# A fused attention and mixture-of-experts kernel: running sums of one-hot vectors moved to TensorE, a cast to GpSimd, an exponential to an earlier step

## The chip, the cores and the metric

The kernel runs on one core of one Trainium2 chip. The metric is the device time of one execution in microseconds (us). A core has five engines with instruction queues of their own: TensorE (PE; its weight loads are listed as PEld), VectorE (DVE), ScalarE (ACT), GpSimd (POOL) and SyncE (SP, which issues most DMAs here). Instructions of one engine start in program order, and engines wait for each other through semaphores.

## The reference

Attention with a bias learned from relative positions, for 8 batches of 8 heads with 576 tokens of 64 channels, then a mixture of 8 experts in which every one of the 4608 tokens goes to the expert with the highest logit.

```python
def _attn_ref(q, k, v, w1, b1, w2):                 # q, k, v: 8 x 8 x 576 x 64
    scores = scale * np.matmul(q, k.transpose(0, 1, 3, 2))
    ...
    bias = np.maximum(x @ w1 + b1, 0.0) @ w2        # x: log distance over log position
    scores = scores + bias.transpose(2, 0, 1)[None, :, :, :]
    attn = np.exp(scores - np.max(scores, axis=-1, keepdims=True))
    attn = attn / (np.sum(attn, axis=-1, keepdims=True) + 1e-09)
    return np.matmul(attn, v)

def _moe_ref(x, modality_id, w_gate, modality_bias, w1, w2):   # x: 4608 x 512
    logits = x @ w_gate + modality_bias[modality_id]
    e_idx = np.argmax(logits, axis=1)
    probs = np.exp(logits - logits.max(-1, keepdims=True))
    probs /= probs.sum(-1, keepdims=True) + 1e-09
    gate_w = probs[np.arange(N), e_idx]
    for e in range(E):                              # 8 experts, 512 -> 1024 -> 512
        mask = e_idx == e
        h = np.maximum(x[mask] @ w1[e], 0.0)
        out[mask] = gate_w[mask, None] * (h @ w2[e])
```

## The kernel before

The program has three phases: a bias table, the attention, and the expert tiles. The attention goes through 32 pairs of heads, four pairs to a batch. One iteration of `attention` over a pair `n` is called a step below; it has five units (`u` = 0 to 4), one per block of 128 query rows (the last block holds the remaining 64 rows of both heads). A unit begins with its score matmuls (`S`: L402 on TensorE); VectorE then adds the bias and takes the row minimum (L416, once per head, into `Eb`), ScalarE does the softmax exponentials (L431), TensorE transposes them (L446), VectorE or ScalarE copies the transposes out (L333, L331, into `eT`), and TensorE multiplies by the values (L500, L491). The next pair's queries and keys are prepared on the way: VectorE transposes them (L378), ScalarE rounds them (L385), and GpSimd subtracts to get the remainder (L386, into `QK`), which the next step's score matmuls read.

The order of everything is written by hand, as the strings of `ORDER`, one letter for an operation, one string for a unit. The letters `X` and `B` stand for the next operation of a queue of background work. After the four pairs of a batch are done, this background work is the batch's routing (`route_steps`), 576 tokens at a time: five groups of up to 128 tokens, 8 experts. Its list `px` (letter `X`) has logits, their transposes, the rank and five times a row scatter; its list `ot` (letter `B`) has reciprocals, the maximum (`s_top`), the one-hot vectors (`s_onehot`), the gate (`s_gate`) and the positions (`s_pos`). A routing so takes about one batch's four steps. Seven of the eight routings run in the attention; the eighth runs beside the first expert tiles (`moe_first`).

Three of these functions, in the order in which they are issued, are touched by the change, and a fourth:

- `s_onehot`, issued at the end of a step's second unit. VectorE makes `oh`, the one-hot vector of each token's expert (L793 to L798, 128 x 5 x 8). GpSimd casts it to bf16 (L801), and VectorE adds up the groups before each group in bf16, five additions of 128 x 8 (L803). Both results stand in `ohb`.
- `s_rank`, in the third unit. TensorE multiplies the cast vectors by a triangular matrix (L816, within a group) and the running sums by ones (L817, groups before). VectorE adds the base of each expert (L820), raises the base (L821) and keeps the entry of the token's own expert (L822).
- `s_gate`, in the third unit. ScalarE exponentiates the logits in place (L807); VectorE adds them up and inverts (L809 to L811) and copies the token numbers (L812).
- `s_pos`, at the start of the fourth unit. VectorE adds over the experts (`pf`, L828) and casts to int32 (`pos`, L830). `s_rows` then transposes 128 rows (L838), copies, scales (L845) and scatters them by `pos` with an indirect DMA (L849), from the fourth unit on.

Of the kernel before, what the change touches and what calls it, by code (L numbers as in the profile page):

```python
# [11 lines left out]
F32 = mybir.dt.float32  # L12
BF16 = mybir.dt.bfloat16
F32R = mybir.dt.float32r
I32 = mybir.dt.int32
AF = mybir.ActivationFunctionType
ALU = mybir.AluOpType
# [4 lines left out]
P = 128  # L22
# [7 lines left out]
E = 8  # L30
# [78 lines left out]
class Attn:  # L109
# [506 lines left out]
    def route_setup(self, cp):  # L616

        tc, nc, io = self.tc, self.nc, self.io
# [13 lines left out]
        nc.gpsimd.memset(self.rec, 1.0)  # L632
        self.oh = cp.tile([P, 6, E], F32, name="oh")
        nc.gpsimd.memset(self.oh, 0.0)
        self.ohb = cp.tile([P, 2, 6, E], BF16, name="ohb")
        nc.gpsimd.memset(self.ohb, 0.0)
        yield
        self.base = cp.tile([P, E], F32, name="base")
# [59 lines left out]
        for a, (dst, mk) in enumerate(((t0, m1), (self.mbias, mf))):  # L698
# [4 lines left out]
                op=ALU.mult,  # L703
# [4 lines left out]
    def route_steps(self, b):  # L708
        nc, rt = self.nc, self.rt
        xT = [self.xT.pop(NP * b + p) for p in range(NP)]  # L710
        sums = [self.sums.pop(NP * b + p) for p in range(NP)]
        rec, oh = self.rec, self.oh
        C5 = [P, 5, E]
        st = {}

        def bc(t):
            return t.rearrange("p (c o) -> p c o", o=1).to_broadcast(C5)
# [71 lines left out]

        def s_onehot():  # L790
            lg, mx = st["lg"], st["mx"]

            nc.vector.scalar_tensor_tensor(  # L793
                oh[:, 0:5, :], lg, 0.0, self.rev.rearrange("p (o e) -> p o e", o=1).to_broadcast(C5), op0=ALU.is_ge, op1=ALU.mult
            )
            nc.vector.tensor_reduce(mx, oh[:, 0:5, :], axis=AX.X, op=ALU.max)
            nc.vector.tensor_tensor(oh[:, 0:5, :], oh[:, 0:5, :], bc(mx), op=ALU.is_equal)
            nc.vector.tensor_tensor(oh[:, 0:5, :], oh[:, 0:5, :], bc(self.valid), op=ALU.mult)  # L798

            ohb = self.ohb  # L800
            nc.gpsimd.tensor_copy(ohb[:, 0, 0:5, :], oh[:, 0:5, :])  # L801
            for k in range(1, 6):
                nc.vector.tensor_tensor(ohb[:, 1, k, :], ohb[:, 1, k - 1, :], oh[:, k - 1, :], op=ALU.add)  # L803

        def s_gate():
            lg = st["lg"]
            nc.scalar.activation(lg, lg, AF.Exp)  # L807
            gt = rt.tile([P, 5], F32, tag="gt", name=f"gt{b}")
            nc.vector.tensor_reduce(gt, lg, axis=AX.X, op=ALU.add)  # L809
            nc.vector.tensor_scalar(gt, gt, 1e-9, None, op0=ALU.add)  # L810
            nc.vector.reciprocal(self.gi[:, :, 0], gt)  # L811
            nc.vector.tensor_copy(self.gi[:, :, 1], self.ids[:, 5 * b : 5 * b + 5])  # L812

        def s_rank():
            ps = self.xbank()[:, 0 : 6 * E].rearrange("p (c e) -> p c e", e=E)
            nc.tensor.matmul(ps, self.tri, self.ohb[:, 0], start=True, stop=False)  # L816
            nc.tensor.matmul(ps, self.ones, self.ohb[:, 1], start=False, stop=True)  # L817
            rk = rt.tile(C5, F32, tag="rk", name=f"rks{b}")
            bb = self.base.rearrange("p (o e) -> p o e", o=1)
            nc.vector.tensor_tensor(rk, ps[:, 0:5, :], bb.to_broadcast(C5), op=ALU.add)  # L820
            nc.vector.tensor_tensor(self.base, self.base, ps[:, 5, :], op=ALU.add)  # L821
            nc.vector.tensor_tensor(rk, rk, oh[:, 0:5, :], op=ALU.mult)  # L822
            st["rk"] = rk

        def s_pos():
            rk = st["rk"]
            pf = rt.tile([P, 5], F32, tag="pf", name=f"pf{b}")
            nc.vector.tensor_reduce(pf, rk, axis=AX.X, op=ALU.add)  # L828
            pos = rt.tile([P, 5], I32, tag="pos", name=f"pos{b}", bufs=2)
            nc.vector.tensor_copy(pos, pf)  # L830
            st["pos"] = pos

        def s_rows(c):
# [22 lines left out]
            return f  # L856

        px = [(1, s_logits(0)), (1, s_logits(1)), (1, s_logits_t(0)), (1, s_logits_t(1)), (3, s_rank)] + [(5, s_rows(c)) for c in range(5)]
        ot = [(0, s_recip), (4, s_top), (4, s_onehot), (4, s_gate), (5, s_pos)]
        if b == self.B - 1:  # L860
            ot += [(5, f) for f in self.last_tables()]
# [595 lines left out]
```

## Time and profile before

| quantity | value |
|---|---|
| device time, median of 3 runs | 1053.26 us (1050.47 to 1053.33) |
| profiled execution, device time | 1052.45 us |
| its span, first to last instruction | 1050.7 us |
| TensorE busy | 997.9 us, 95% |
| VectorE busy | 764.5 us, 73% |
| ScalarE busy | 666.8 us, 63% |
| GpSimd busy | 304.7 us, 29% |
| mean granted TensorE clock | 0.995 |

The profile is that of one execution. Durations of instructions, waits and the order of events come from it; the other runs give the median. An engine's busy share is a mean over stages that differ, so the stage in question has to be looked at by itself. A matmul's record covers its whole way through the array, so that records of successive matmuls overlap; the distance between two starts tells what one costs.

### The profile page before, as it was taken

The numbers are of one execution on the slowest core, as the hardware profiler recorded it, in microseconds if no ns is written. First come the engines' busy times: TensorE is split into PE (matmuls) and PEld (weight loads), VectorE is DVE, ScalarE is ACT, GpSimd is POOL, SyncE is SP. The second block draws the span as 40 slices with busy tenths as digits, with TensorE's granted clock in tenths as the row PEclk, the third lists the DMA queues.
The fourth block names the chain that finished last, engine by engine and source line by source line (L and its number), as shares of the span: only waits on it lengthen the run. The fifth ranks groups of instructions, "written<-read, shape, count | busy, mean of one in ns | idle before, by whom it ended". The sixth has DMA issues, their size and how long they took to land. (4 is left out here: it accounts for less than half of the span.)

```text
span 1050.7 us, 22872 instructions
## 1 busy us (share of the span) xinstructions
PE 997.9 (95%) x8236; PEld 786.4 (75%) x8236; DVE 764.5 (73%) x1566; ACT 666.8 (63%) x1265; POOL 304.7 (29%) x489
## 2 busy tenths in 40 slices
PE   6789999998999999999999899999999999999997
PEld 2347766776767767676677678988999999898886
DVE  8886678778787786877879767797566676565555
ACT  6777776776767767677677655555455555554544
POOL 1512333525335244253352411441110111111111
PEclk9999999999999999999999999999999999999999
DMA  6977723233334323352325511122215641170610
GB/s 150 191 154 146 189 54 73 68 69 78 72 56 93 66 59 74 55 110 50 79 60 103 166 36 41 61 67 71 61 51 120 220 133 51 41 224 26 226 40 26
DMA packets 247325, 97.50 MB, mean 93 GB/s; under 512 B 207759, under 2 KB 228623, under 8 KB 247203
## 3 DMA queue, kind: packets, MB, share of 16 engines
q1 hardware_dynamic: 241186, 76.92, 32.9%
q0 software_dynamic: 5920, 19.03, 5.0%
q8 instruction: 67, 1.10, 0.4%
q14 instruction: 56, 0.45, 0.1%
q10 hardware_dynamic: 96, 0.00, 0.0%
HBM read 134.90 MB, written 23.90 MB: 151 GB/s over the span
## 5 line engine op out<-in xcount | busy, mean ns | idle before, releaser
L431 ACT ACTIVATE Eb<-Eb,mn 128x576 f32<-128x576 f32 x288 | 221.2, 769 | 66.1 <-DVE mn L416 63.3
L416 DVE CUSTOM_DVE_ANT_0 Eb<-sps,NBm 128x576 f32<-128x576 f32 x256 | 183.6, 754 | 62.2 <-PE sps L402 56.2
L402 PE MATMUL sps<-QK 64*128 64x288 f32 (+1 forms) x1728 | 171.1, 309 | 2.0 <-DVE mn L416 1.7
L402 PEld LDWEIGHTS sps<-QK 64*128 64x128 f32 (+1 forms) x1728 | 133.8, 185 | 45.8 <-DVE mn L416 15.5
L1181 PE MATMUL p<-QK,w1hi 128*128 128x256 f32 x1136 | 161.5, 285 | 1.7 <-DVE QK L1165 0.9
L446 PE MATMUL eps<-idf,Eb 128*128 128x128 f32 x1024 | 147.8, 279 | 10.6 <-DVE eT L333 8.3
L1181 PEld LDWEIGHTS p<-QK,w1hi 128*128 128x128 f32 x1136 | 147.0, 191 | 5.4 <-issue 1.8
L500 PE MATMUL xps<-eT,vraw 128*64 128x288 f32 x1024 | 148.7, 416 | 0.0
L446 PEld LDWEIGHTS eps<-idf,Eb 128*128 128x128 f32 x1024 | 111.2, 141 | 41.8 <-issue 17.8
L1207 POOL DMA_INDIRECT out<-mo,idt x36 | 41.4, 1151 | 301.4 <-ACT mo L1206 228.2
L1184 DVE SCALAR_TENSOR_TENSOR hl<-p,hh 128x512 fp32r<-128x512 f32 x72 | 49.7, 690 | 101.4 <-ACT hh L1183 97.8
L1183 ACT ACTIVATE hh<-p 128x512 fp32r<-128x512 f32 x72 | 43.0, 597 | 122.1 <-PE p L1181 106.7
L331 ACT ACTIVATE eT<-eps 128x512 f32<-128x512 f32 x160 | 94.7, 592 | 34.7 <-PE eps L446 26.3
L1198 PE MATMUL p<-w2hi,hl 128*128 128x512 f32 x288 | 112.4, 390 | 0.3 <-DVE hl L1184 0.3
L1198 PE MATMUL p<-w2hi,hh 128*128 128x512 f32 x288 | 112.4, 390 | 0.0
L436 POOL COPY rem<-Eb 128x128 f32<-128x128 f32 x128 | 37.5, 293 | 249.6 <-ACT Eb L431 246.6
L500 PEld LDWEIGHTS xps<-eT,vraw 128*64 128x64 f32 x1024 | 65.9, 138 | 54.1 <-issue 20.5
L1143 DVE TENSOR_TENSOR w2lo<-NBm,w2hi 128x1024 fp32r<-128x1024 f32 x72 | 88.1, 1224 | 15.9 <-ACT w2hi L1142 15.9
L333 DVE COPY eT<-eps 128x512 f32<-128x512 f32 x128 | 87.1, 681 | 12.0 <-PE eps L446 11.5
L1181 PE MATMUL p<-QK,w1lo 128*128 128x256 f32 x568 | 91.3, 283 | 0.0
L1143 DVE TENSOR_TENSOR w1lo<-NBm,w1hi 128x1024 fp32r<-128x1024 f32 x72 | 83.3, 1220 | 0.0
L1181 PEld LDWEIGHTS p<-QK,w1lo 128*128 128x128 f32 x568 | 78.3, 192 | 0.0
(213 smaller groups left out, 1574.8 us busy)
## 6 DMA issues: line engine op xcount, KB each, us to landing
NBm<-moe_w SPq DMA_DIRECT2D x44, 1024.0 KB
NBm<-moe_w SPq DMA_DIRECT2D x80, 512.0 KB
NBr<-xg SPq DMA_DIRECT2D x80, 128.0 KB
kraw<-k SPq DMA_DIRECT2D x128, 72.0 KB
NBm<-xTb SPq DMA_DIRECT2D x32, 288.0 KB
vraw<-v SPq DMA_DIRECT2D x64, 128.0 KB
NBm<-moe_w SPq DMA_DIRECT2D x3, 2048.0 KB
xg<-blank SPq DMA_DIRECT2D x9, 516.0 KB
```

The source lines that it names most:

```text
L331: self.nc.scalar.activation(out, ps, AF.Copy, scale=scale)
L333: self.nc.vector.tensor_copy(out, ps)
L402: nc.tensor.matmul(self.sps[h][:, half, 0:HS], QK[o, q, qs], QK[o, k, HS * half : HS * half + HS], start=i == 0, stop=i == 2, skip_group_c ...
L416: nc.vector.tensor_tensor_reduce(out=e.rearrange("p (t w) -> p t w", t=2), in0=self.sps[h][:, :, 0:HS], in1=nb.rearrange("p (t w) -> p t w ...
L431: self.nc.scalar.activation(e, e, AF.Exp, bias=mn, scale=-1.0, accum_out=sm)
L446: nc.tensor.transpose(ps[:, k, :], e[:, part, P * k : P * k + P], self.idf)
L500: nc.tensor.matmul(ps[o, :], v[:, h, k, :], self.eT[:, h, k, sl], start=half == 1 and k == 0, stop=half == 0 and k == 3, tile_position=(0, ...
L1143: self.nc.vector.tensor_tensor(l, w, h.bitcast(F32), op=ALU.subtract)
L1181: nc.tensor.matmul(ps[:, a, :], w[:, c, fs], x[:, c, :], start=i == 0, stop=i == len(ops) - 1)
L1183: nc.scalar.activation(hh[:, sl, :], ps, AF.Relu)
L1184: nc.vector.scalar_tensor_tensor(hl[:, sl, :], ps, 0.0, hh[:, sl, :].bitcast(F32), op0=ALU.max, op1=ALU.subtract)
L1198: nc.tensor.matmul(ps, h[:, f, sl], m[:, f, :], start=i == 0, stop=i == len(ops) - 1)
```

## The change

- `ohb` holds the bf16 one-hot vectors alone. VectorE's product with the mask of valid tokens writes them directly; GpSimd's cast and the five additions on VectorE are gone.
- The rank is one product with the triangular matrix and five products with ones: group `k` of the one-hot vectors, repeated by a stride of zero, is added into the results of all later groups, so that the accumulation in PSUM makes the running sums.
- The exponentials of the gate are written to a tile of their own (`eg`), and are issued in `s_onehot`.
- The position cast is GpSimd's instead of VectorE's.

```diff
-        self.ohb = cp.tile([P, 2, 6, E], BF16, name="ohb")
+        self.ohb = cp.tile([P, 6, E], BF16, name="ohb")
...
         def s_onehot():
             lg, mx = st["lg"], st["mx"]
-
+            st["eg"] = eg = rt.tile(C5, F32, tag="eg", name=f"eg{b}")
+            nc.scalar.activation(eg, lg, AF.Exp)
...
-            nc.vector.tensor_tensor(oh[:, 0:5, :], oh[:, 0:5, :], bc(self.valid), op=ALU.mult)
-
-            ohb = self.ohb
-            nc.gpsimd.tensor_copy(ohb[:, 0, 0:5, :], oh[:, 0:5, :])
-            for k in range(1, 6):
-                nc.vector.tensor_tensor(ohb[:, 1, k, :], ohb[:, 1, k - 1, :], oh[:, k - 1, :], op=ALU.add)
+            nc.vector.tensor_tensor(self.ohb[:, 0:5, :], oh[:, 0:5, :], bc(self.valid), op=ALU.mult)
 
         def s_gate():
-            lg = st["lg"]
-            nc.scalar.activation(lg, lg, AF.Exp)
+            lg = st["eg"]
...
         def s_rank():
             ps = self.xbank()[:, 0 : 6 * E].rearrange("p (c e) -> p c e", e=E)
-            nc.tensor.matmul(ps, self.tri, self.ohb[:, 0], start=True, stop=False)
-            nc.tensor.matmul(ps, self.ones, self.ohb[:, 1], start=False, stop=True)
+            ohb = self.ohb
+            nc.tensor.matmul(ps, self.tri, ohb, start=True, stop=False, skip_group_check=True)
+            for k in range(5):
+                nc.tensor.matmul(
+                    ps[:, k + 1 : 6, :],
+                    self.ones,
+                    ohb[:, k : k + 1, :].to_broadcast([P, 5 - k, E]),
+                    start=False,
+                    stop=k == 4,
+                    skip_group_check=True,
+                )
...
-            nc.vector.tensor_tensor(rk, rk, oh[:, 0:5, :], op=ALU.mult)
+            nc.vector.tensor_tensor(rk, rk, self.ohb[:, 0:5, :], op=ALU.mult)
...
-            nc.vector.tensor_copy(pos, pf)
+            nc.gpsimd.tensor_copy(pos, pf)
```

VectorE's queue around the one-hot vectors, before: the end of the second unit, then L416, with which the third unit begins (`mn` and `Eb` are its results).

```order
L333 COPY rT<-eps_717 128x64
L793 SCALAR_TENSOR_TENSOR oh<-lgs_1917,rev 128x40
L796 TENSOR_REDUCE mx_1939<-oh 128x5
L797 TENSOR_TENSOR oh<-oh,mx_1939 128x40
L798 TENSOR_TENSOR oh<-oh,valid 128x40
L803 TENSOR_TENSOR ohb<-ohb,oh 128x8 x5
L416 ISA Eb,mn_2_0_2033<-sps_714,NBm 128x576
```

The same place after the change.

```order
L333 COPY rT<-eps_717 128x64
L794 SCALAR_TENSOR_TENSOR oh<-lgs_1917,rev 128x40
L797 TENSOR_REDUCE mx_1939<-oh 128x5
L798 TENSOR_TENSOR oh<-oh,mx_1939 128x40
L799 TENSOR_TENSOR ohb<-oh,valid 128x40
L416 ISA Eb,mn_2_0_2029<-sps_714,NBm 128x576
```

Five additions have left the queue ahead of L416; nothing else moved there. On the same queue the cast L830, between `pf` (L828) and the fourth unit's L416, is gone too.

GpSimd's queue from the second to the fourth unit, before (`rem` is a copy of the last 64 columns of `Eb`, `QK` the remainders that the next step reads).

```order
L801 CAST ohb<-oh 128x40
L436 COPY rem_1_2015<-Eb 128x128
L386 TENSOR_TENSOR QK_73<-qT,QK_73 128x640
L436 COPY rem_2_2065<-Eb 128x128
L386 TENSOR_TENSOR QK_73<-kT,QK_73 128x576
L845 TENSOR_TENSOR xrb_90<-xrb_90,rec 128x512
```

The same place after the change.

```order
L436 COPY rem_1_2011<-Eb 128x128
L386 TENSOR_TENSOR QK_73<-qT,QK_73 128x640
L436 COPY rem_2_2064<-Eb 128x128
L834 CAST pos_2072<-pf_2070 128x5
L386 TENSOR_TENSOR QK_73<-kT,QK_73 128x576
L849 TENSOR_TENSOR xrb_90<-xrb_90,rec 128x512
```

The cast of the one-hot vectors has left the queue ahead of the query remainder, and the position cast stands now ahead of the key remainder.

## Rows read from the trace of the kernel before

**Rows 1.** The page's first part: busy time, share of the span, instructions.
```profile
PE 997.9 (95%) x8236; PEld 786.4 (75%) x8236; DVE 764.5 (73%) x1566; ACT 666.8 (63%) x1265; POOL 304.7 (29%) x489
```

**Rows 2.** Who waited for whom: total us, times, longest.
```profile
PE xps L817 <- DVE ohb L803: 11.4, 7, 1.6
```

**Rows 3.** Stretches: us, busy of PE, PEld, DVE, ACT, POOL, clock, DMA, GB/s.
```profile
178.33:195.13 16.80, 16.50 (x151) 12.36 (x150) 12.52 (x28) 12.05 (x29) 10.55 (x16) 1.00 0.41 97
...
227.53:246.57 19.04, 16.49 (x149) 12.34 (x148) 17.07 (x49) 12.73 (x31) 5.80 (x9) 1.00 0.33 57
```

**Rows 4.** TensorE's timeline, step with the rank: start, us, then [idle before <-releaser].
```profile
234.13 1.05 PE L402 MATMUL sps<-QK 64*128 64x288 f32 x12
...
236.05 0.19 PE L816 MATMUL xps<-ohb,tri 128*128 128x48 bf16 x1
237.86 0.18 PE L817 MATMUL xps<-ohb,ones 128*128 128x48 bf16 x1 [1.63 <-DVE ohb L803]
...
239.10 1.25 PE L402 MATMUL sps<-QK 64*128 64x288 f32 x12
...
243.17 1.05 PE L402 MATMUL sps<-QK 128*128 128x288 f32 x6
245.14 1.06 PE L446 MATMUL eps<-idf,Eb 128*128 128x128 f32 x8 [0.92 <-DVE eT L333]
```

**Rows 5.** TensorE's timeline in the step from 178.33: fourth and fifth unit.
```profile
188.49 1.05 PE L402 MATMUL sps<-QK 64*128 64x288 f32 x12
...
192.37 1.03 PE L402 MATMUL sps<-QK 128*128 128x288 f32 x6
193.70 1.06 PE L446 MATMUL eps<-idf,Eb 128*128 128x128 f32 x8 [0.30 <-ACT Eb L431]
```

**Rows 6.** Stretch of a third unit with no routing matmul, columns as above.
```profile
201.74:204.88 3.14, 3.14 (x30) 2.17 (x28) 2.31 (x7) 3.02 (x8) 1.78 (x2) 1.00 0.00 0
```

**Rows 7.** VectorE's timeline in the step with the rank.
```profile
235.17 0.20 DVE L798 TENSOR_TENSOR oh<-oh,valid 128x40 f32<-128x40 f32 x1
235.40 2.41 DVE L803 TENSOR_TENSOR ohb<-ohb,oh 128x8 bf16<-128x8 bf16 x5
237.79 0.76 DVE L416 CUSTOM_DVE_ANT_0 Eb<-sps,NBm 128x576 f32<-128x576 f32 x1
...
239.85 0.16 DVE L820 TENSOR_TENSOR rks<-xps,base 128x40 f32<-128x40 f32 x1
...
241.63 0.82 DVE L830 CAST pos<-pf 128x5 int32<-128x5 f32 x1
242.36 0.74 DVE L416 CUSTOM_DVE_ANT_0 Eb<-sps,NBm 128x576 f32<-128x576 f32 x1
```

**Rows 8.** GpSimd's timeline there: both remainders.
```profile
235.85 1.53 POOL L386 TENSOR_TENSOR QK<-qT,QK 128x640 fp32r<-128x640 f32 x1
...
240.99 1.44 POOL L386 TENSOR_TENSOR QK<-kT,QK 128x576 fp32r<-128x576 f32 x1 [0.21 <-ACT QK L385]
```

**Rows 9.** One line's instructions: shortest/median/longest ns, first and last start.
```profile
L803 DVE TENSOR_TENSOR ohb<-ohb,oh x5: 167/168/1468, 235.4 to 237.6; 128x8 bf16<-128x8 bf16 x5
...
L817 PEld LDWEIGHTS <-ones x8: 97/98/100, 167.8 to 650.6; 128*128 128x128 bf16 x8
```

**Rows 10.** Timelines of VectorE and TensorE at the eighth routing.
```profile
649.35 0.98 DVE L803 TENSOR_TENSOR ohb<-ohb,oh 128x8 bf16<-128x8 bf16 x5
...
665.41 0.17 DVE L830 CAST pos<-pf 128x5 int32<-128x5 f32 x1
...
650.58 0.20 PE L816 MATMUL xps<-ohb,tri 128*128 128x48 bf16 x1
650.62 0.18 PE L817 MATMUL xps<-ohb,ones 128*128 128x48 bf16 x1
```

**Rows 11.** ScalarE's timeline in the step with the rank.
```profile
238.59 0.78 ACT L431 ACTIVATE Eb<-Eb,mn 128x576 f32<-128x576 f32 x1 [2.19 <-DVE mn L416]
...
239.37 0.22 ACT L807 ACTIVATE lgs<-lgs 128x40 f32<-128x40 f32 x1
```

## The prediction

> **What bounds the kernel now.** I read the busy shares first. TensorE is busy for 95% of the span [rows 1] and its granted clock in the steps below is 1.00, the 2.4 GHz level [rows 3], so time is to be won only where TensorE stands still. The list of waits names such a place on the lines of this change: the second rank product (L817) waits 11.4 us in 7 waits for VectorE's running sums (L803) [rows 2]. The eighth routing, in the expert phase, has no such wait.
>
> Next I compared the steps of the attention loop. The step from 178.33 and the step from 227.53, which carry different parts of a routing, have the same TensorE time, 16.50 and 16.49 us. They last 16.80 and 19.04 us [rows 3]. The second is the one with the one-hot, rank and position code, and it leaves TensorE idle for 2.55 us. There are seven such steps, one in every four from the seventh step on. A step has five units, each opened by its score matmuls (L402). In this step the third unit lasts 239.10 - 234.13 = 4.97 us, the fourth 243.17 - 239.10 = 4.07, and the fifth, up to the step's end at 246.57, 3.40 [rows 3, 4]. In the step that began at 178.33, with as many row transposes in its fourth and fifth unit, these two last 192.37 - 188.49 = 3.88 and 195.13 - 192.37 = 2.76 [rows 3, 5]. A third unit with no routing matmul lasts 3.14 [rows 6]. The step with the rank is thus 2.55 us idle in two places: 1.63 us before L817 and 0.92 us in its fifth unit, before transposes that wait for a VectorE copy [rows 4]. The comparison step has 0.30 us at the latter place, and there it waits for ScalarE [rows 5].
>
> Why VectorE is late is in its own rows. The five running sums take 2.41 us, and the position cast 0.82 us [rows 7]. GpSimd's subtraction of the query remainder (L386) runs from 235.85 to 237.38, that of the key remainder from 240.99 to 242.43 [rows 8]. The cast ends at 242.45, 0.02 us after the latter. Of the five sums one took 1468 ns against a median of 168 [rows 9]. In the eighth routing, where no such subtraction runs, the five take 0.98 us together and the cast 0.17 [rows 10]. So two VectorE instructions per routing stand until a GpSimd instruction ends: 1.43 us in the sums, 0.65 in the cast.
>
> **The change, part by part.**
>
> *The running sums go from VectorE to TensorE.* VectorE loses 2.41 us in each of seven routings. After the product with the valid mask (start 235.17, 0.20 us) it can begin the next score pass (L416) at about 235.44 instead of 237.79 [rows 7]. TensorE reaches the first rank product at 236.05 [rows 4], 0.7 us after the one-hot vectors are written, so it need not wait there. Of the 4.97 us, 1.63 are the wait and 3.14 the unit's own; the two products cost 4.97 - 1.63 - 3.14 = 0.20. Four more products are added, each with a weight load of its own. The trace has no row of five small products in succession. From below, L816 and L817 start 0.04 us apart where the weights were already there [rows 10]; from above, one record of L816 is 0.19 us [rows 4]. I take the weight load's 98 ns [rows 9], since 8 to 40 columns are fewer than the 48 of that 0.04 us and the load is then the longer part. That is 4 x 0.098 = 0.39 us, between 0.16 and 0.76. The third unit becomes 3.14 + 0.20 + 0.39 = 3.73 us; gain 4.97 - 3.73 = 1.24.
>
> *What is late next.* VectorE starts L416 about 1.31 us after the unit's score matmuls; two passes and the key transpose follow, which in the trace take from 237.79 to 239.85, so rank sums begin at +3.37. From there to the next L416 the trace has 242.36 - 239.85 = 2.51 us, of which 0.82 is the cast [rows 7]; without it L416 comes at about +3.37 + 1.69 = +5.06. TensorE's next score matmuls begin at +3.73 and take 1.05 us, so VectorE is then at most 0.3 us behind instead of 2 to 3. The fourth and fifth unit should then be those of the comparison step, 3.88 and 2.76: gains of 0.19 and 0.64. The 0.30 us on ScalarE stays.
>
> *The position cast goes to GpSimd.* It stands there ahead of the subtraction of the key remainder, which before needed nothing from VectorE. It waits for the sum pf (about +5.1, from the reckoning above) and takes about 0.2 us (the eighth routing's cast on VectorE: 0.17 [rows 10]); the subtraction then runs from about +5.4 to +6.85. The matmuls that need it open the next step at +3.73 + 3.88 + 2.76 = +10.4, so 3.5 us of cover are left. Costed at nothing. If the cover were gone, every microsecond would be lost on TensorE.
> The Trainium skill (Perfetto Trace Analysis, Optimizing Scalar/DVE Operations) warns that GpSimd and VectorE share a port, so that moving an operation between them might not help. By that warning the 0.19 us of the fourth unit would not come, and the sum would be 1.3 us higher, near 1040. The row speaks for the move all the same: the cast was held by GpSimd's own subtraction, and in GpSimd's queue it stands before it.
>
> *GpSimd's cast of the one-hot vectors goes away*; it held nothing that TensorE waits for, so no term. *The exponential* (0.22 us on ScalarE [rows 11]) is issued one unit earlier, between two softmax exponentials; its input is already there. It puts ScalarE's next work 0.22 us later and gives it back in the next unit. In the old place ScalarE had been idle for 2.19 us just before its neighbour [rows 11]; with VectorE earlier it will not be, so up to 0.22 us per routing could show. I take none, since the only wait of TensorE for ScalarE in the comparison step lies two units later [rows 5]. The bf16 operand of the rank product on VectorE has one price (the same 40 columns), no term.
>
> *The eighth routing* lies in the expert phase, where TensorE runs without a gap around 650.6 [rows 10]. VectorE's savings bring nothing there, and TensorE pays 0.39 us.
>
> **Sum.** Seven routings at 1.24 + 0.19 + 0.64 = 2.07 us are 14.5 us; less 0.39 makes 14.1. The profiled execution took 1052.45 us (span 1050.7, 1.75 around it): 1038.4. The median of the three runs is 0.8 above the profiled one, so I forecast **1039 us**. A second reckoning agrees: the rank step's TensorE time of 16.49 plus 0.39 plus 0.30 idle is 17.2 us instead of 19.04, a gain of 12.9 over seven, about 1040.
>
> **Rivals.**
>
> *Only the named wait goes* (1045 us). The later units keep their 0.19 and 0.64 because VectorE is still late: it keeps four one-hot instructions before L416 and nine short ones after the transpose. For it: in the fifth unit VectorE is the releaser. Against it: VectorE wins 3.06 us more than TensorE's 1.24 would need. Gain 7 x 1.24 - 0.4 = 8.3, so 1044 to 1045; with the products at their upper price 7 x 0.87 - 0.8 = 5.3, so 1047.
>
> *The hold moves to another instruction, so the change does not do what it says* (1053 us). The multiplication that now writes the bf16 one-hots has two SBUF operands, like the held sums. If the query remainder began before it ends, it would stand until 237.38, and six products after it would begin about 0.2 us sooner than L817 does now and cost 0.39 more. Before, it ends 0.48 us ahead of that subtraction (235.37 against 235.85), and the earlier exponential moves the subtraction 0.22 us further off. The gains of the later units would go with it: 1053, within 0.3%.
> This is the rule of the Trainium skill (SBUF — State Buffer, Who interferes with whom): a VectorE instruction with two SBUF inputs contends with a GpSimd instruction that reads SBUF, and whichever comes second waits for the whole of the other. The trace agrees in both held instructions; the page's rule by itself does not say which instruction meets which.
>
> *GpSimd becomes the one waited for* (slower). The cast holds the key remainder until pf is there, and the next step's scores wait for it. This costs nothing until pf comes 3.5 us later than reckoned; it eats the gain of 2.07 after 5.6 us, and from about 6 us late each routing is over 0.46 us slower, 1056 us or more. pf depends on VectorE alone, which has gained 3 us, so this is unlikely.
>
> **How the numbers follow.** Forecast 0.74, only the named wait 0.16, the hold moves 0.06, GpSimd late 0.04. The forecast's own range is 1036 to 1042: products between 0.16 and 0.76 us are 1.6 us less to 2.6 more, ScalarE's 0.22 is 1.5 more, and runs of one kernel differ by up to 2.9. To hold 8 in 10 it must take in the first rival: 1035.5 to 1047. A measurement of this kernel can tell about 0.3% (3 us). Faster by more than that: 0.90; within it 0.06; slower 0.04.
>
> **What the changed profile would show.** Right: no wait of TensorE for one-hots; a step with a rank of about 17.0 us, with units of 3.7, 3.9 and 2.8; L416 about 1.3 us behind the score matmuls of the third unit; VectorE's busy time in that step down by some 3 us from 17.07 [rows 3]; the cast on GpSimd at about 0.2 us and the key subtraction ended more than 3 us before the next step. Wrong: TensorE waiting for VectorE's masked one-hots (the hold moved), for ScalarE or for GpSimd's remainder at a step's start; added products pitched well over 0.1 us; or a fifth unit still at 3.4.

## The result, and the profile after

The changed kernel takes 1033.52 us, the median of four runs (1033.21 to 1035.74), and the kernel before took 1053.15 in the four runs beside them: a ratio of 0.9824, interval 0.9803 to 0.9845. It is faster, as forecast, and by 5.5 us more than forecast: the time lies 2 us under the low end of the range. The two profiled executions are 1052.45 and 1033.21 us long, 19.24 us apart. TensorE is now busy for 97% of the span, 995.6 us against 997.9; the page's first part:

```profile
PE 995.6 (97%) x8268; PEld 786.2 (76%) x8268; DVE 743.1 (72%) x1518; ACT 665.4 (65%) x1265; POOL 306.3 (30%) x489
```

The stretches that answer to [rows 3] follow: first a whole step with a rank, then one without (it was 16.80), then the third, fourth and fifth unit of the first step. The columns are the stretch and its length, the busy time of PE, PEld, DVE, ACT and POOL, the granted clock, the DMA share and GB/s.

```profile
223.53:239.98 16.45, 16.20 (x153) 12.22 (x152) 14.16 (x43) 12.46 (x31) 5.87 (x9) 1.00 0.35 62
174.35:191.16 16.81, 16.51 (x152) 12.37 (x151) 12.52 (x28) 12.05 (x29) 10.68 (x16) 1.00 0.43 101
230.13:233.38 3.25, 3.25 (x36) 2.42 (x34) 3.15 (x11) 3.25 (x9) 1.75 (x2) 1.00 0.01 3
233.38:237.27 3.89, 3.89 (x38) 2.89 (x37) 3.17 (x15) 2.24 (x7) 2.01 (x4) 1.00 0.14 31
237.27:239.98 2.71, 2.46 (x21) 2.09 (x19) 1.90 (x4) 2.03 (x6) 1.81 (x3) 1.00 0.62 120
```

A step with a rank lasted 19.04 us and now lasts 16.46, with the units' starts taken as TensorE's timeline has them: the third unit fell from 4.97 to 3.26, the fourth from 4.07 to 3.89, the fifth from 3.40 to 2.71. That is 2.58 us; all seven steps with a rank agree within 0.04 us, so it makes 18.1 over the seven, nearly the whole 19.24. The step without a rank is as long as before. Where the 1.71 us of the third unit went is in TensorE's timeline (start, us, line, operation, [idle before <-releaser]), which answers to [rows 4]:

```profile
230.13 1.05 PE L402 MATMUL sps<-QK 64*128 64x288 f32 x12
...
232.04 0.19 PE L812 MATMUL xps<-ohb,tri 128*128 128x48 bf16 x1
232.07 0.27 PE L814 MATMUL xps<-ohb,ones 128*128 128x40 bf16 x5
232.26 1.19 PE L500 MATMUL xps<-eT,vraw 128*64 128x288 f32 x8
...
238.55 1.06 PE L446 MATMUL eps<-idf,Eb 128*128 128x128 f32 x8 [0.25 <-ACT Eb L431]
```

All six products start between 232.04 and 232.26, where the next work starts: 0.22 us after the first of them. In the kernel before the first rank product started at 236.05 [rows 4] and the next work started here:

```profile
237.98 1.19 PE L500 MATMUL xps<-eT,vraw 128*64 128x288 f32 x8
```

So the rank held TensorE for 1.93 us, and for 0.22 now. The wait that is left in the fifth unit is ScalarE's, as in the comparison step of [rows 5].

VectorE's timeline answers to [rows 7]. The masked one-hots are written by 231.40, the next score pass (L416) starts 1.22 us after the unit's score matmuls (237.79 - 234.13 = 3.66 us in [rows 4, 7]), and no cast stands ahead of the one at 235.07:

```profile
231.16 0.24 DVE L799 TENSOR_TENSOR ohb<-oh,valid 128x40 bf16<-128x40 f32 x1
231.35 0.76 DVE L416 CUSTOM_DVE_ANT_0 Eb<-sps,NBm 128x576 f32<-128x576 f32 x1
...
234.97 0.18 DVE L832 TENSOR_REDUCE pf<-rks 128x5 f32<-128x40 f32 x1
235.07 0.75 DVE L416 CUSTOM_DVE_ANT_0 Eb<-sps,NBm 128x576 f32<-128x576 f32 x1
```

On GpSimd, in the answer to [rows 8], the cast takes 0.19 us and the key remainder behind it ends at 236.80, 3.2 us before the step at 239.98 that needs it:

```profile
231.93 1.59 POOL L386 TENSOR_TENSOR QK<-qT,QK 128x640 fp32r<-128x640 f32 x1 [0.57 <-ACT QK L385]
...
235.22 0.19 POOL L834 CAST pos<-pf 128x5 int32<-128x5 f32 x1 [0.88 <-DVE pf L832]
235.37 1.43 POOL L386 TENSOR_TENSOR QK<-kT,QK 128x576 fp32r<-128x576 f32 x1
```

### The profile page after: what moved, and what is told of

Same layout as the page of the kernel before. It is cut to its first block, busy times and chain, and to the rows that moved or that the text cites. A ratio compares the mean times of both kernels' runs of the same rounds, so it can differ in the third digit from the quotient of the medians.

```text
span 1031.4 us, 22903 instructions
## 1 busy us (share of the span) xinstructions
PE 995.6 (97%) x8268; PEld 786.2 (76%) x8268; DVE 743.1 (72%) x1518; ACT 665.4 (65%) x1265; POOL 306.3 (30%) x489
## 5 line engine op out<-in xcount | busy, mean ns | idle before, releaser
L416 DVE CUSTOM_DVE_ANT_0 Eb<-sps,NBm 128x576 f32<-128x576 f32 x256 | 183.6, 755 | 62.2 <-PE sps L402 53.9
```

Of the source, the lines that this page charges most:

```text
L416: nc.vector.tensor_tensor_reduce(out=e.rearrange("p (t w) -> p t w", t=2), in0=self.sps[h][:, :, 0:HS], in1=nb.rearrange("p (t w) -> p t w ...
```

## The experiments

The theory that went on trial: two VectorE instructions per routing stood still until a GpSimd instruction ended (a hold, below), one among the five running sums and the position cast, and the gain is that both are gone. The rivals were that the gain is TensorE's new way of summing, or the cast alone, or the exponential's new place, and that a product costs a full weight load. Each run has its own runs of the kernel before beside it (medians of 1051.7 to 1052.3 us).

### The products without the rest

Kernel before, with the six products alone; the five sums go, the cast stays on VectorE and the exponential stays where it was.

```diff
-            for k in range(1, 6):
-                nc.vector.tensor_tensor(ohb[:, 1, k, :], ohb[:, 1, k - 1, :], oh[:, k - 1, :], op=ALU.add)
...
-            nc.tensor.matmul(ps, self.tri, self.ohb[:, 0], start=True, stop=False)
-            nc.tensor.matmul(ps, self.ones, self.ohb[:, 1], start=False, stop=True)
+            ohb = self.ohb[:, 0]
+            nc.tensor.matmul(ps, self.tri, ohb, start=True, stop=False, skip_group_check=True)
+            for k in range(5):
+                nc.tensor.matmul(ps[:, k + 1 : 6, :], self.ones, ohb[:, k : k + 1, :].to_broadcast([P, 5 - k, E]), ...)
```

> The kernel before with one part of the change: the running sums as five products on TensorE. GpSimd's cast of the one-hots, VectorE's position cast and the place of the exponential are as before. Theory 'hold': the wait before the rank is gone and the third unit is 3.3 us as in the changed kernel; the position cast may still stand behind GpSimd's key remainder, but VectorE is early enough by then, so nearly all of the gain: 1034 to 1038 us. Rival 'cast' (the fourth and fifth unit gained because the cast left VectorE): third unit 3.3, fourth and fifth stay at about 4.1 and 3.4, total 1040 to 1042 us.

Measured: 1034.52 us (1033.43 to 1035.89), ratio 0.9837 (0.9814 to 0.9859). The third, fourth and fifth unit as stretches:

```profile
230.42:233.68 3.26, 3.26 (x36) 2.43 (x35) 3.16 (x11) 3.18 (x9) 1.96 (x3) 1.00 0.01 3
233.68:237.57 3.89, 3.89 (x39) 2.89 (x37) 3.75 (x14) 2.01 (x5) 1.73 (x3) 1.00 0.14 33
237.57:240.55 2.98, 2.46 (x22) 2.09 (x21) 2.07 (x6) 2.50 (x7) 1.82 (x3) 1.00 0.58 112
```

and the instructions of the cast's line (shortest, median, longest ns; first and last start):

```profile
L837 DVE CAST pos<-pf x8: 173/920/965, 169.6 to 647.9; 128x5 int32<-128x5 f32 x8
```

The cast is held as before, 920 ns in the median, and still the third and fourth unit are those of the changed kernel and the fifth is 2.98: with the sums gone VectorE has slack enough to carry a held cast with little loss. The rival 'cast' missed.

### The cast without the rest, and the change without the cast

First the kernel before with one word changed.

```diff
-            nc.vector.tensor_copy(pos, pf)
+            nc.gpsimd.tensor_copy(pos, pf)
```

> The kernel before with one part of the change: the position cast on GpSimd. The running sums stay on VectorE and are held as before, so the third unit stays at 4.97 us. Theory 'hold': VectorE is 0.82 us earlier at the fourth unit's score pass but still over 1.5 us late from the third; the fourth and fifth unit give back a part, 0.2 to 0.8 us together: 1047 to 1052 us. Rival 'cast': they give back all of 0.87 us: about 1047 us. Both allow 1047, so the units tell: fifth unit at 2.7 with the cast alone, or about 3.0.

Measured over nine runs: 1047.42 us (1045.03 to 1052.12), ratio 0.9968 (0.9952 to 0.9984). The three units:

```profile
231.51:236.48 4.97, 3.33 (x33) 2.32 (x31) 4.70 (x14) 2.69 (x6) 1.96 (x3) 1.00 0.00 0
236.48:240.56 4.08, 4.08 (x39) 3.07 (x37) 3.90 (x17) 2.96 (x10) 1.82 (x3) 1.00 0.14 32
240.56:243.27 2.71, 2.46 (x22) 2.09 (x20) 1.90 (x4) 2.07 (x6) 1.88 (x4) 1.00 0.59 116
```

With the sums still held, the cast's move brings the fifth unit down from 3.40 to 2.71 and leaves the third and fourth untouched: the fifth unit's loss needs the held cast, the fourth unit's does not. The total fits both theories, but the fifth unit's 2.71 is the figure of the rival, not the 3.0 of 'hold': I had taken VectorE to be still late there. The fourth unit gave back nothing, so the rival's 0.87 did not come either. Then the changed kernel with the cast put back on VectorE, the same edit the other way round:

> The changed kernel with the position cast back on VectorE. Theory 'hold': the key remainder now starts before the cast, so the cast again takes 0.7 to 0.8 us; VectorE is early enough for that, the fourth and fifth unit change by 0.2 us at most: 1033 to 1035.5 us. Rival 'cast': fourth and fifth unit go back to about 4.1 and 3.4 us, seven times 0.9: about 1040 us.

Measured: 1035.22 us (1034.44 to 1035.65), ratio 0.984 (0.9819 to 0.986). Units of 3.26 and 3.88, and the fifth at 2.86 against 2.71; the cast is held again, 824 ns in the median. The fifth unit as a stretch:

```profile
238.05:240.91 2.86, 2.46 (x21) 2.09 (x19) 1.97 (x6) 2.37 (x7) 1.81 (x3) 1.00 0.62 120
```

So with the products the two savings overlap: the cast's move is worth 0.69 us per step by itself and 0.15 behind them (0.27, from 2.98 to 2.71, if the run before is compared with the whole change).

### The sums on VectorE, with one operand each

Kernel before, where each running sum is a reduction over the one-hots, with one operand instead of two. No product is moved.

```diff
-                nc.vector.tensor_tensor(ohb[:, 1, k, :], ohb[:, 1, k - 1, :], oh[:, k - 1, :], op=ALU.add)
+                nc.vector.tensor_reduce(ohb[:, 1, k, :], oh[:, 0:k, :].rearrange("p c e -> p e c"), axis=AX.X, op=ALU.add)
```

> The kernel before, except that each of the five running sums is a reduction over the one-hot groups before it: still five VectorE instructions of 128 x 8 in the same place, but with one operand read from SBUF instead of two. Theory 'hold' (VectorE loses the time standing until GpSimd's query remainder ends, because its instruction reads two SBUF operands): no sum of about 1.47 us, the five take about 1.0 us instead of 2.41, TensorE's wait before the second rank product falls from 1.63 to about 0.2 us, the step with the rank from 19.04 to 16.7 to 17.5 us; total 1038 to 1043 us. Rival 'work' (the five instructions themselves cost the time, whatever their operands): as before, 1050 to 1054 us.

Measured: 1036.31 us (1035.82 to 1039.68), ratio 0.9863 (0.9836 to 0.9889). The third, fourth and fifth unit as stretches:

```profile
230.88:234.05 3.17, 3.17 (x32) 2.32 (x31) 3.03 (x16) 2.81 (x6) 1.87 (x3) 1.00 0.00 0
234.05:238.00 3.95, 3.95 (x39) 2.95 (x37) 3.81 (x16) 2.10 (x7) 1.84 (x3) 1.00 0.14 32
238.00:241.40 3.40, 2.48 (x21) 2.11 (x20) 2.49 (x6) 2.87 (x7) 1.82 (x3) 1.00 0.62 115
```

and VectorE's timeline there, the five reductions in one row:

```profile
232.15 0.57 DVE L804 TENSOR_REDUCE ohb<-oh 128x8 bf16<-128x8 f32 x5
...
236.46 0.82 DVE L831 CAST pos<-pf 128x5 int32<-128x5 f32 x1
```

The wait before the rank is gone, and the fifth unit stays at 3.40 because the cast is still held. The step lasts 17.12 us, within what I expected, and the total lies 1.7 us under the range. The five reductions take 0.57 us, less than I had expected; why is not shown. They are nearly through when the subtraction starts (232.59), which leaves it open whether their form or the shorter time saved them; two runs further down show that a reduction is not held even while the subtraction runs.

### Both holds removed, and nothing moved to TensorE

The reductions of the last run and the cast on GpSimd together.

> The kernel before with two edits and no product moved to TensorE: the five running sums as reductions with one SBUF operand (still on VectorE), and the position cast on GpSimd. Theory 'hold': the third unit is 3.2 us as with one-operand sums alone, the fourth about 3.9, the fifth 2.7 as with the cast alone; the step with the rank 16.3 to 16.6 us, total 1031 to 1034 us, the time of the changed kernel. Rival 'work' (the sums have to leave VectorE): the fifth unit stays at 3.4 and the total at 1036 us.

Measured over five runs: 1032.97 us (1032.18 to 1034.67), ratio 0.9823 (0.9803 to 0.9843). The step and its three units:

```profile
224.80:241.24 16.44, 16.20 (x150) 12.20 (x150) 14.65 (x48) 12.66 (x31) 5.99 (x10) 1.00 0.35 61
231.41:234.58 3.17, 3.17 (x32) 2.32 (x31) 3.03 (x16) 2.82 (x6) 1.87 (x3) 1.00 0.01 1
234.58:238.53 3.95, 3.95 (x39) 2.95 (x37) 3.78 (x17) 2.83 (x10) 1.93 (x4) 1.00 0.13 30
238.53:241.24 2.71, 2.47 (x22) 2.10 (x21) 1.90 (x4) 2.07 (x6) 1.89 (x4) 1.00 0.62 121
```

The whole gain is there with the two old products. What TensorE does for the sums is one way to take VectorE's adds out of the way, and no part of the gain. Here the two savings do not overlap but add: 1.92 us for the reductions alone (19.04 to 17.12) and 0.69 for the cast alone make 2.61, and the step is 2.60 shorter. With the reductions and a held cast, VectorE's next score pass starts 3.14 us after the fourth unit's score matmuls (237.19 - 234.05); with the products and a held cast it was 2.66 (236.34 - 233.68), early enough to make up most of it.

### An added instruction with two operands, and one with one

Changed kernel, with one small VectorE instruction added to each of the seven routings, between the two score passes of the third unit, where the query remainder is running: once a 128x8 addition with two operands in SBUF, once a 128x8 reduction with one. Nothing reads what it writes.

```diff
+            if h == 0 and self.poke:
+                f, self.poke = self.poke, None
+                f()
...
+                self.poke = lambda: nc.vector.tensor_tensor(pk, self.rev, self.rev, op=ALU.add)
```

The second run has this in place of the last line:

```diff
+                self.poke = lambda: nc.vector.tensor_reduce(pk[:, 0:1], self.rev, axis=AX.X, op=ALU.add)
```

> The changed kernel with one more VectorE addition of 128 x 8 in seven routings, between the two score passes of the third unit, while GpSimd's query remainder runs. It reads two SBUF operands and writes a tile that nothing reads. Theory 'hold': it stands until the remainder ends, about 1.4 us instead of 0.17; the second score pass comes 1.5 us later, TensorE waits about 1 us for its PSUM bank in the fourth unit, and the fifth unit may lose up to 0.6 more: 1040 to 1046 us. Rival 'work': 0.2 us of VectorE time that nobody waits for: 1033 to 1035 us.

> As the run with the additional addition of two operands, but the additional instruction is a reduction of 128 x 8 with one SBUF operand, in the same place. Theory 'hold': it takes about 0.17 us and nobody waits: 1033 to 1035 us. Rival (any short instruction there is late, for another reason than its second operand): as with two operands, 1040 us or more.

Measured: 1038.44 us (1037.45 to 1041.99), ratio 0.9882 (0.986 to 0.9903), for two operands, and 1034.4 (1033.11 to 1034.98), 0.9835 (0.9818 to 0.9851), for one. In the former, the instructions of the added line:

```profile
L806 DVE TENSOR_TENSOR pk<-rev x7: 1469/1479/1494, 166.2 to 566.3; 128x8 f32<-128x8 f32 x7
```

the subtraction in GpSimd's timeline:

```profile
232.63 1.58 POOL L387 TENSOR_TENSOR QK<-qT,QK 128x640 fp32r<-128x640 f32 x1 [0.57 <-ACT QK L386]
```

the addition in VectorE's:

```profile
232.74 1.49 DVE L806 TENSOR_TENSOR pk<-rev 128x8 f32<-128x8 f32 x1
```

the score matmuls that wait in TensorE's:

```profile
234.97 1.05 PE L403 MATMUL sps<-QK 64*128 64x288 f32 x11 [0.48 <-DVE mn L417]
```

and the fourth unit as a stretch:

```profile
234.09:238.84 4.75, 4.27 (x38) 3.06 (x37) 4.58 (x18) 2.57 (x7) 1.92 (x4) 1.00 0.10 24
```

In the latter, the instructions of the added line:

```profile
L806 DVE TENSOR_REDUCE pk<-rev x7: 155/156/156, 166.0 to 560.8; 128x1 f32<-128x8 f32 x7
```

The addition starts 0.11 us after the subtraction and ends at 234.23, 0.02 us after it (232.63 + 1.58 = 234.21), and all seven are as long; the reduction in the same place takes 156 ns and leaves the units at 3.26, 3.88 and 2.71. The hold is shown, and that it depends on the instruction's form: an addition with two operands stands, a reduction with one doesn't. That the number of operands alone decides is not shown, and the position cast speaks against it: it reads one operand and was held in every version that had it on VectorE. The hold's price is smaller than I had expected, and the total lies 1.6 us under the range: 0.87 us in the fourth unit and none in the fifth. The addition comes after the one-hots, and no rank product waits for it.
The Trainium skill (SBUF — State Buffer, Who interferes with whom) says the same: two SBUF inputs contend with a GpSimd instruction that reads SBUF, a reduction on this chip never does, and the order of issue decides which of the two waits. The traces agree on the first two, with 1479 against 156 ns; the added addition always came second and waited, and the other order was not tried.

### Twenty more products

Changed kernel with twenty further products of the same kind per routing, ahead of the six, into PSUM columns that nothing reads.

```diff
+            for k in list(range(5)) * 4:
+                nc.tensor.matmul(spare[:, k + 1 : 6, :], self.ones, ohb[:, k : k + 1, :].to_broadcast([P, 5 - k, E]), ...)
```

> The changed kernel with 20 more products with ones in each of the eight routings (each of the five forms four times more, with its weight load, into PSUM columns that nothing reads). It measures the price of such a product by itself. If they follow each other every 0.025 us, as the five of the changed kernel seem to: 0.5 us per routing, 1036.5 to 1038.5 us. If a weight load of 0.098 us each has to pass: 2 us per routing, about 1049 us.

Measured: 1038.54 us (1037.44 to 1039.76), ratio 0.9878 (0.9856 to 0.9899). The third unit as a stretch:

```profile
231.05:234.81 3.76, 3.76 (x58) 2.92 (x56) 3.62 (x15) 3.76 (x11) 1.87 (x2) 1.00 0.03 7
```

and TensorE's timeline in it:

```profile
232.96 0.65 PE L815 MATMUL xps<-ohb,ones 128*128 128x40 bf16 x20
233.46 0.18 PE L823 MATMUL xps<-ohb,tri 128*128 128x48 bf16 x1
...
233.69 1.19 PE L500 MATMUL xps<-eT,vraw 128*64 128x288 f32 x8
```

From 232.96 to 233.46 twenty products start in 0.50 us, 0.025 each, and the unit is 0.50 longer. The median lies at the upper end of the first range, far from 1049. Their weight loads still have records of 95 to 100 ns, but these lie beside one another and say nothing of the pitch. Over eight routings the products make 4 us, and the runs differ by 5.0. By this pitch the four products of the change cost 0.10 us, not the 0.39 that I took.
The Trainium skill (TensorE: Matmul & The Clock Gate, Wait — 56ns, not 53.3ns?) states that starts of small matmuls never come closer than about 25 ns; the run agrees, with a weight load in each of the twenty.

### The exponential in its old place, twice, and the changed kernel again

Changed kernel with the exponential put back into the gate's code and its old tile.

```diff
-            st["eg"] = eg = rt.tile(C5, F32, tag="eg", name=f"eg{b}")
-            nc.scalar.activation(eg, lg, AF.Exp)
...
-            lg = st["eg"]
+            lg = st["lg"]
+            nc.scalar.activation(lg, lg, AF.Exp)
```

> The changed kernel with the exponential of the gate in place and at its old position, one step later. If its position matters, VectorE waits for ScalarE before the gate's sum and the step grows by 0.2 to 0.5 us: 1035 to 1037 us. If it doesn't, the time is that of the changed kernel within 1 us: 1032.5 to 1035 us. I expect the latter.

Measured: 1031.94 us (1030.46 to 1032.92), ratio 0.9805 (0.9789 to 0.9822). That lies under both ranges and looked 1.6 us better than the changed kernel, with no shorter step with a rank. So both ran once more, on one chip:

> The changed kernel with the exponential in place and at its old position, once more and beside the changed kernel. The rank steps are the same by the earlier profile (16.46 us), so the same time within 1 us. If the difference of 1.6 us between the two medians was real, it shows again.

> The changed kernel once more, as the measure for the runs beside it: 1033 to 1035 us, the step with the rank 16.45 us.

Measured: 1033.74 us (1031.37 to 1035.81), ratio 0.9827 (0.9803 to 0.9851), with the exponential in its old place, and 1033.84 (1032.39 to 1035.68), 0.9828 (0.9807 to 0.985), as changed. The step with a rank lasts 16.45 us in the first of these runs and 16.47 in the second and third. The third, the changed kernel again, as a stretch:

```profile
225.60:242.07 16.47, 16.22 (x153) 12.23 (x152) 14.18 (x43) 12.45 (x31) 5.85 (x9) 1.00 0.34 61
```

The exponential's place is worth nothing that can be measured, and the 1.6 us between two medians of four runs did not show again.

### The first subtractions on VectorE

In the changed kernel's profile the first score matmul starts 1.5 us earlier than before (66.03 against 67.54), ahead of any routing. GpSimd's two subtractions for the first pair lie there, one with a record of 16.23 us:

```profile
20.14 1.75 POOL L386 TENSOR_TENSOR QK<-qT,QK 128x640 fp32r<-128x640 f32 x1 [18.22 <-ACT QK L385]
...
26.72 16.23 POOL L386 TENSOR_TENSOR QK<-kT,QK 128x576 fp32r<-128x576 f32 x1 [3.85 <-ACT QK L385]
```

I put both on VectorE for that pair, to see whether this sets the start and the scatter.

```diff
-        nc.gpsimd.tensor_tensor(lo, x, hi.bitcast(F32), op=ALU.subtract)
+        (nc.vector if n == 0 else nc.gpsimd).tensor_tensor(lo, x, hi.bitcast(F32), op=ALU.subtract)
```

> The changed kernel, but the two remainders of the first pair of heads, which are made during the bias table, are subtracted on VectorE instead of GpSimd. In the profiles so far GpSimd's subtraction of the key remainder takes about 15 us there, and one or two of VectorE's bias instructions take 1.1 to 2.1 us instead of 0.5. Theory 'hold': those go, VectorE pays two instructions of about 0.7 us; the first score matmuls come at 64.5 to 66 us in every run, and the runs scatter less: 1031.5 to 1034 us. Rival: VectorE is the bound in the bias table and pays in full: 1034 to 1036 us.

Measured: 1035.03 us (1032.23 to 1037.54), ratio 0.9843 (0.9819 to 0.9867). The subtractions take 0.83 and 0.76 us on VectorE, but the first score matmul starts at 66.87 and the runs scatter no less. This missed: with the subtractions gone from GpSimd the start lies where it lay in other runs (65.27 to 67.97 over all 14 profiles).

## Why the prediction was right in its mechanism and wrong in its time

**What bounds the kernel: right in the main.** TensorE's idle time in the steps with a rank was most of what there was to win. Of 2.55 us per step 0.25 is left, ScalarE's, against the 0.30 that I had left standing. But time was not to be won from idle time only: TensorE's busy time in the step fell as well, from 16.49 to 16.20 us, though four products were added (0.09 in the third unit, 0.18 in the fourth). The score matmuls that opened the fourth unit, for one, had a record of 1.25 us against 1.05 in the third [rows 4], and now have one of 1.06. The second reckoning kept the 16.49 and added 0.39 to it, so its step came out at 17.2 us, further from the measured 16.46 than the first reckoning's 16.97.

**The held sums: right in kind, and the mis-sized term.** The step that failed is the price of the rank products on TensorE. The forecast made the third unit 3.14 + 0.20 + 0.39 = 3.73 us, and it is 3.26. Both the 0.20 and the 0.39 were too high. The unit with the two old products and no wait takes 3.17 (the run with one-operand sums), so these two cost 0.03, not 0.20; the unit with six takes 3.26, so four more cost 0.09, not 0.39. Together that is 0.47 us in each of seven steps, 3.3 of the 5.1 us by which the profiled execution beat its sum, and 0.3 more in the eighth routing, where the first product and the next work are some 0.1 us further apart than before, not 0.39.

Why they were too high: for the 0.20 I subtracted the idle time of 1.63 us in front of L817 from the unit. But the idle time is counted from the end of L816's record, and this record is 0.19 us long while the next instruction can start 0.03 us after it (232.04 and 232.07 in the timeline after). What the wait had cost in starts is 4.97 - 3.17 = 1.80. For the 0.39 I took the length of a weight load's record as the distance of two of them; [rows 10], with 0.04 us between two starts, was the nearer row, and I used it as a bound only, in the belief that the weights were already there. They were not. TensorE's weight loads at that place:

```profile
650.59 0.10 PEld L817 LDWEIGHTS <-ones 128*128 128x128 bf16 x1
```

The load starts 0.03 us ahead of its product at 650.62, and its record ends after that product has started. So the 0.04 us had a load in it, and was no bound from below: the five products of the changed kernel start 0.025 us apart. The range's low end did carry 0.16 for the four products, but treated the 0.20 as certain.

**What is late next: right.** L416 starts 1.22 us after the third unit's matmuls (I had 1.31), and the next unit's scores meet VectorE in time. The fourth unit gained 0.18 (I had 0.19), the fifth 0.69 (0.64).

**The cast: right.** It takes 0.19 us on GpSimd, and 3.2 us of cover are left of the 3.5 reckoned. The experiments add what the sum could not tell: the fifth unit's 0.69 and the products' gain overlap, and behind the products only 0.15 to 0.27 of it is the cast's own. The warning against the move was not borne out, and I had put its price in the wrong unit: the cast alone brought 0.69 us in the fifth unit and nothing in the fourth, where I had looked for 0.19. Nor does the rule for two inputs, which I set beside both held instructions, cover the cast, which reads one.

**The exponential, the bf16 operand and GpSimd's dropped cast: right at nothing**, by the two pairs of runs for the first. The write of the bf16 one-hots takes 0.24 us, where the write it replaces took 0.20.

**The rivals.** That only the named wait goes fell with the units of 3.89 and 2.71. That the hold moves to the multiplication for the bf16 one-hots did not come about: it ends at 231.40, 0.53 us ahead of the subtraction at 231.93. Its mechanism is real, as the added addition showed. GpSimd is not late. The argument against the first rival has a slip: 3.06 us (2.41 + 0.65) is all that VectorE wins, and not what it wins beyond the 1.24.

**What is left.** With the products at their measured price the sum is 1052.45 - 7 x (1.71 + 0.19 + 0.64) + 0.1 = 1034.8 us on the profiled run and 1035.5, the range's low end, on the median of 1053.15: the mis-sized price takes the forecast from 1039 to the edge of the range. The profiled 1033.21 is 1.6 lower still. Of that the fifth unit's 0.05 makes 0.35. The start of the attention loop lay 1.5 us earlier, which is not the change's doing: the same code ran again with its first score matmul at 67.97. Another step of the loop was 0.5 us longer (16.82 against 16.31), by the table instruction told of at the end.

What sets the start from one execution to the next stays open. In the three profiles in which it is latest (67.51 to 67.97) TensorE's granted clock was at its 1.2 GHz level just before, 0.50 from 63.80 to 67.20 in the kernel before; but so it was in four that start earlier, the changed kernel's among them.

The base of the forecast was high, too: in the 28 runs beside the experiments the kernel before took 1051.7 to 1052.3 us in the median, and from there the sum with the measured price gives 1034.0 to 1034.6, within 1.1 us of the 1033.5 and 1033.8 that the changed kernel took.

## What to carry to other kernels

Look for small instructions whose longest record is many times the median and ends with an instruction of another engine: such a hold can cost several times the instruction's own time (1.47 us against 0.17 here). Two remedies removed it here without new work: writing additions of two operands as reductions, and moving the instruction into the queue of the engine that holds it. A single operand alone is no safeguard, as the cast shows. Price tiny matmuls by the distance between starts, never by the length of a record of theirs, of a weight load, or of the idle time between records. When an engine gets slack, the next holds on it can become cheap, so two savings measured alone need not add: with the products they overlapped, with the reductions they added. Measure them together.

## What the runs showed of the chip beyond that

**TensorE drops to its lower level in some executions.** At the end of the attention loop TensorE stands idle for 2.00 us before L452 (1.6 to 2.0 in the other versions). In 8 of 14 profiles of these kernels its granted clock is then at the 1.2 GHz level for a while, in the others not. The kernel before had it, in TensorE's timeline:

```profile
608.87 0.66 PE L452 MATMUL eps<-idf,Eb 128*128 128x128 f32 x4 [2.00 <-ACT eT L331]
610.03 2.14 PE L500 MATMUL xps<-eT,vraw 128*64 128x288 f32 x8
...
615.66 0.66 PE L491 MATMUL xps<-rT,vrem 128*64 128x288 f32 x4
```

and in a stretch there, at a granted clock of 0.51:

```profile
609.90:613.30 3.40, 3.40 (x22) 1.84 (x18) 1.10 (x3) 0.00 (x0) 0.09 (x1) 0.51 0.10 23
```

The kernel with both holds removed had not, in TensorE's timeline:

```profile
590.58 0.65 PE L452 MATMUL eps<-idf,Eb 128*128 128x128 f32 x4 [2.01 <-ACT eT L331]
591.70 1.14 PE L500 MATMUL xps<-eT,vraw 128*64 128x288 f32 x8
...
595.70 0.66 PE L491 MATMUL xps<-rT,vrem 128*64 128x288 f32 x4
```

and in a stretch there, at 1.00:

```profile
591.00:595.00 4.00, 4.00 (x39) 2.35 (x38) 1.78 (x4) 1.04 (x3) 0.76 (x5) 1.00 0.17 37
```

The same matmuls take 615.66 - 610.03 = 5.63 us at the lower level and 4.00 at the higher: 1.6 us. With the cast alone moved, one execution showed it in the attention loop too, at a granted clock of 0.50 after the 1.67 us wait of L817, where a fourth unit took 5.59 us instead of 4.07. So a wait can cost TensorE more than its own length, in some executions. That this makes part of the 2 to 4 us by which most runs of one kernel differ is likely, not shown, since only the profiled executions have a trace. The mean granted clock speaks for it; of the nine runs of the cast alone the slowest (1052.12 us) had 0.990 and the fastest (1045.03) 0.996.

**A hold needs no size.** In the changed kernel's profile a table instruction with two operands, of one partition and five elements, stood for 1.42 us until the key remainder ended, and TensorE waited 0.56 us for an addition that came later in VectorE's queue. VectorE's timeline:

```profile
547.69 1.42 DVE L1015 TENSOR_TENSOR tabf<-tabf 1x5 f32<-1x5 f32 x1
```

and GpSimd's:

```profile
547.68 1.42 POOL L386 TENSOR_TENSOR QK<-kT,QK 128x576 fp32r<-128x576 f32 x1 [0.22 <-ACT QK L385]
```

With the exponential in its old place the cast two instructions later was held there instead, for 1.43 us, and TensorE did not wait. One such chance meeting is left in each of the 14 profiles.
